# The gate's products on TensorE, beside the arriving weights, in a fused attention, dense and routed layer kernel

## The chip, the cores and the metric

The kernel runs on one core of one Trainium2 chip. The metric is the device time of one execution in microseconds. Engines are TensorE (PE; its weight loads are listed as PEld), VectorE (DVE), ScalarE (ACT), GpSimd (POOL) and SyncE (SP, which here only issues DMAs).

## The reference

Three parts follow each other: gated linear attention, a dense layer pair with squared ReLU, and eight routed experts.

```python
# attention, 4 batches x 8 heads, 768 tokens, 48 columns a head
for t in range(S):
    state = alpha[:, :, t, :, None] * state + einsum('bhd,bhe->bhde', k[:, :, t], v[:, :, t])
    y[:, :, t] = einsum('bhd,bhde->bhe', q[:, :, t], state)
x = y.transpose(0, 2, 1, 3).reshape(3072, 384)
# first mixture
h = maximum(x @ w_in, 0.0)             # w_in 384 x 2048
x = h * h @ w_out                      # w_out 2048 x 384
# second mixture: each expert takes the 384 tokens with the highest logits that are still free
logits = x @ w_gate                    # w_gate 384 x 8
order = argsort(-logits.flatten())
... each token to one expert, 384 tokens to an expert ...
for e in range(8):
    out[mask_e] = maximum(x[mask_e] @ w1[e], 0.0) @ w2[e]     # w1 384 x 1024, w2 1024 x 384
```

## The kernel before

**Units and steps.** The 3072 tokens are 24 chunks of 128; three chunks are a unit (`CPU`, `UT` = 384 tokens), so there are 8 units. The hidden 2048 columns are 16 blocks of 128 (`FT`). A step g is a unit u and a block f, g = 16 u + f. On TensorE step g computes the first layer of block g (`moe_a`, line 390, nine products of 128 x 128 by 128 x 384) and the second layer of block g - 2 (`moe_b`, line 414, nine products). Each value is split into a high and a low float32r part, and a product is three passes over these. Between the two layers lies `moe_ev`: ScalarE's ReLU (line 395), the square (ScalarE in unit 0, VectorE's line 400 in the others), ScalarE's high part (line 401) and GpSimd's low part (line 402).

**Attention** of the next unit runs beside a unit's steps, in pieces (`attn`: decays with two scans on VectorE, lines 229 and 232; scaled keys and queries, 236 and 237; scores on TensorE and masks on VectorE, 255 and 261; keys transposed, 295; results and state, 273, 276, 306 and 312). Three pieces go with four steps. Its PSUM banks come from tag `"a"`, of which there are three.

**Unit 0** is written in order by hand for TensorE, VectorE, ScalarE and GpSimd (`manual_schedule`), up to two steps into unit 1 (`first_step`). In it the first mixture's weights arrive as float64 words, and VectorE narrows them to float32 in three instructions for each block of `w_in` (`conv_in`) and of `w_out` (`conv_out`): lines 351, 353 and 355. Two conversions are started at the end of each step (`start_conv`), the blocks of the first layer two steps ahead of their use. In the next step they are split into high (ScalarE, line 358) and low (GpSimd, line 359). All this keeps the order of the text on each engine. From step 18 on the order is the scheduler's.

**The gate.** The logits are needed before routing starts. For units 0 to 4 VectorE multiplies each chunk's rows (`xo`) by the gate's eight columns, one instruction with a running sum for each expert (`gate`, line 435, a second instruction reads the sum out). From unit 5 (`FUSED`) the second layer's products carry them: `gate_w` multiplies the rows of `w_out` by the gate's weights in the same way (128 such sums, GpSimd adding the two parts into `gx`, line 442) and puts the results as 8 columns beside `w_out`'s 384 (`W` = 392). `share` hands out four steps of this work per step of the units. For that the gate's weights are loaded once, spread to all partitions (`wg`, 128 x 8 x 384). The last unit's logits come from `wlog` and its hidden rows.

**After that** come the search for the experts' thresholds and the experts themselves, in an order by hand.

Of the kernel before, what the change touches and what calls it, by code (L numbers as in the profile page):

```python
# [48 lines left out]
# what each step of an expert does beside its products: s the search of a phase after the next, t the slots  # L49
# of the next, h, p, d weights' parts, x tokens, e, w the former expert's results  # L50
# [21 lines left out]
FUSED = 5  # L72
SHARE = 4
# [14 lines left out]
def moe_kernel(ctx: ExitStack, tc: tile.TileContext, akq, v, w_in, w_out, w_gate, w1, w2, out,  # L88
# [14 lines left out]
    # the last chunk's rows come after one of zeros  # L103
# [14 lines left out]
    # attention inputs of one chunk of 128 tokens: decays, keys and queries with a pair of heads' columns in the  # L118
    # partitions, a column of zeros after each pair's tokens, and values with the tokens in the partitions
# [3 lines left out]
    def load(ch, parts=((0, 3),), eng=sp):  # L123
        """the rows between a pair's heads take the second's first, for whatever is finite will do"""
        for lo, hi in parts:
            for p0, n, r0 in ((0, 64, 0), (64, 48, 48)):
                eng.dma_start(nat[ch % 2][p0:p0 + n, lo:hi, :, :C], akq[ch, r0:r0 + n, lo:hi])
# [4 lines left out]
    # constants that the first chunk needs  # L132
# [30 lines left out]
    # constants that depend on shapes alone  # L163
# [15 lines left out]
    wlog = consts.tile([128, FT, 2, E], F32R, name="wlog")  # L179

# [28 lines left out]
    XF, XT = {}, {}  # L209

    def back(x):
        """a row's elements, the last one first"""
        n = x.shape[-1]
        return bass.AP(tensor=x.tensor, offset=x.offset + n - 1, ap=[list(a) for a in x.ap[:-1]] + [[-1, n]])

    def attn(ch, tags="aaaaa"):
        """yields after each of its parts: a decays, q queries and keys, s scores, n keys back, o results"""
# [7 lines left out]
        # products of the decays from each token on, and up to each token over the whole chunk's; what each pair's  # L225
        # start from comes in where the zeros are
# [41 lines left out]
        def result(lo, hi):  # L268
            """what some pairs of heads give, in one bank"""
# [10 lines left out]
            if cu == CPU - 1 and hi == NP:  # L280
                # the last pair of heads fills the rows that the other pairs leave
# [65 lines left out]
    def narrow(dst, src):  # L347
        """float64 words (low, high) to float32, of which dst takes the bits"""
# [23 lines left out]
    def conv_out(f):  # L372
# [6 lines left out]
        split(lambda i: wout[:, i, f, :DM].rearrange("p (k q) -> p k q", k=KT), r)  # L379
        yield  # L380

# [25 lines left out]
    def moe_b(u, f):  # L407
# [3 lines left out]
        w = W if FUSED <= u < NU - 1 else DM  # L411
# [5 lines left out]
    def moe_out(u, wp):  # L417
        for t in range(CPU):
# [4 lines left out]
            if u >= FUSED:  # L423
                dve.tensor_copy(L[:, c, :], p[:, DM:W])
            else:
                tasks.append(gate(L[:, c, :], xo))
            sp.dma_start(rows(c), xo)

    tasks = []

    def gate(dst, x):
        """x's rows times the gate's weights"""
        for e in range(E):
            junk = gt_.tile([128, DM], F32, name="gj", bufs=1)
            dve.scalar_tensor_tensor(junk, x, 1.0, wg[:, e], op0=OP.mult, op1=OP.mult, accum_out=dst[:, e:e + 1])  # L435
            yield

    def gate_w():
        """w_out's rows times the gate's weights"""
        for f in range(FT):  # L440
            x = gt_.tile([128, DM], F32, name="gx", bufs=2)
            pool.tensor_tensor(x, wout[:, 0, f, :DM].bitcast(F32), wout[:, 1, f, :DM].bitcast(F32), op=OP.add)
            yield from gate(wr[:, f], x)
        split(lambda i: wlog[:, :, i], wr)
        for i in range(2):
            pool.tensor_copy(wout[:, i, :, DM:], wlog[:, :, i])
        yield

    def share(n):
        """n steps of what the vector engine does for the gate"""  # L450
        while n and tasks:
            if next(tasks[-1], "end") == "end":
                tasks.pop()
            else:
                n -= 1

# [14 lines left out]
    def start_conv(n=1):  # L471
        """the next conversions, in turns so that none waits for itself"""
# [13 lines left out]
    for what in ORDER:  # L486
# [15 lines left out]
        if what == "0q":  # L502
# [4 lines left out]
            load_out(0)  # L507
            load_in(1)
# [8 lines left out]
    def logit_range():  # L517
        """the lowest of the logits, but for the last unit's, and what scales them from there to 0..T"""
# [25 lines left out]
    def attend(g):  # L544
        """attention's parts that go with step g"""
# [11 lines left out]
    def first_step(g):  # L557
        """a step of the first unit, whose weights come along"""
# [13 lines left out]
        if g >= 2:  # L572
            moe_b(0, g - 2)
        if g == FT + 1:
            moe_out(0, mp_)
# [9 lines left out]
    gt_, gt_stack = open_pool("gate")  # L585
    wg = gt_.tile([128, E, DM], F32, name="wg")
    sp.dma_start(wg, bass.AP(tensor=w_gate.tensor, offset=w_gate.offset, ap=[[0, 128], [DM, E], [1, DM]]))
    wr = gt_.tile([128, FT, E], F32, name="wr")
    tasks.insert(0, gate_w())

# [665 lines left out]
```

## Time and profile before

| | us |
|---|---|
| median of 3 runs | 973.15 |
| lowest, highest | 966.78, 974.82 |
| span of the profiled execution (its own time is known by the span) | 973.9 |
| TensorE busy | 833.9 |
| VectorE busy | 714.5 |
| GpSimd busy | 443.2 |
| ScalarE busy | 327.7 |

The span runs from the first to the last instruction of the profiled execution. A busy share is a mean over stages that have different limits; a busy TensorE is not TensorE at its peak, since its products are pipelined and the ends of their records are modelled. Times in the rows further down are counted from the span's start.

### The profile page before, as it was taken

What the parts mean: (1) busy time and instruction counts of PE and PEld (TensorE: products, weight loads), DVE (VectorE), ACT (ScalarE), POOL (GpSimd) and SP (SyncE); (2) the same over time, 40 slices, a digit from 0 to 9 for tenths busy, and PEclk for the clock granted to TensorE, in tenths of its full rate; (3) what the DMA queues carried; (4) which work ended last, traced back from release to release, by engine and by line L of the source; (5) the groups of instructions that cost most, each with busy time, mean ns of one, the idle gap of its engine ahead of it and who ended that gap; (6) DMA issues with size and microseconds to landing.
All of it is one profiled execution on the core that took longest, in us unless ns stands there. A gap on an engine that the chain in (4) does not pass through costs nothing.

```text
span 973.9 us, 14629 instructions
## 1 busy us (share of the span) xinstructions
PE 833.9 (86%) x5583; PEld 759.1 (78%) x5583; DVE 714.5 (73%) x1594; ACT 327.7 (34%) x581; POOL 443.2 (46%) x389
## 2 busy tenths in 40 slices
PE   6868779888979889899999999748788797988974
PEld 6658678877878779899999998647677685777974
DVE  6878998999998999958542134777687787875540
ACT  1344533223123223233343352224242442425521
POOL 2386763353454444433342442343464556644431
PEclk7888989999999999999999999958798898988988
DMA  9763543112122122232300000314042240422400
GB/s 208 156 190 107 164 110 70 37 28 61 38 43 62 37 43 61 37 72 56 58 25 1 7 25 13 134 37 155 1 178 102 77 171 9 178 84 96 179 25 27
DMA packets 51484, 76.98 MB, mean 79 GB/s; under 512 B 3409, under 2 KB 42706, under 8 KB 49362
## 3 DMA queue, kind: packets, MB, share of 16 engines
q1 hardware_dynamic: 21570, 27.24, 10.3%
q0 software_dynamic: 5520, 34.61, 9.6%
q10 hardware_dynamic: 24320, 14.16, 7.7%
q8 instruction: 45, 0.74, 0.3%
q14 instruction: 29, 0.24, 0.1%
HBM read 65.27 MB, written 9.54 MB: 77 GB/s over the span
## 4 chain that ended last, share of the span: by engine, by line
PE 40%; DVE 36%; issue 4%; ACT 4%; DMA 1%; POOL 1%; POOLq 0%; DVEq 0%; ACTq 0%
DVE gj L435 15%; PE ph L390 9%; PE p L414 7%; PE ph L957 7%; PE py L975 7%; DVE at L861 3%; PE p L641 3%; DVE s L400 3%; DVE wbuf L922 2%; ACT wbuf L920 2%; DVE A L232 1%; DVE thr L827 1%; DVE cm L829 1%; DVE suf L229 1%; DVE Pt L261 1%
## 5 line engine op out<-in xcount | busy, mean ns | idle before, releaser
L390 PE MATMUL ph<-xT,wbuf 128*128 128x384 f32 x1152 | 234.6, 348 | 29.5 <-DVE s L400 12.0
L390 PEld LDWEIGHTS ph<-xT,wbuf 128*128 128x128 f32 x1152 | 207.5, 192 | 40.4 <-DVE s L400 17.4
L402 POOL TENSOR_TENSOR hl<-s,hl 128x384 fp32r<-128x384 f32 x112 | 141.8, 1266 | 184.9 <-ACT hl L401 171.2
L414 PE MATMUL p<-wbuf,hl 128*128 128x384 f32 (+1 forms) x1008 | 205.4, 348 | 4.9 <-POOL hl L402 2.7
L414 PEld LDWEIGHTS p<-wbuf,hl 128*128 128x128 f32 x1008 | 180.0, 193 | 12.2 <-issue 4.2
L975 PE MATMUL py<-wbuf,hl 128*128 128x384 f32 x576 | 133.6, 364 | 0.0
L957 PE MATMUL ph<-xt,wbuf 128*128 128x384 f32 x576 | 122.5, 358 | 10.3 <-DVE xt L932 5.9
L400 DVE SCALAR_TENSOR_TENSOR s<-ph,s 128x384 f32<-128x384 f32 x112 | 62.0, 553 | 89.2 <-ACT s L395 88.8
L401 ACT ACTIVATE hl<-s 128x384 fp32r<-128x384 f32 x112 | 58.8, 525 | 195.7 <-DVE s L400 193.8
L957 PEld LDWEIGHTS ph<-xt,wbuf 128*128 128x128 f32 x576 | 103.7, 198 | 14.1 <-DVE xt L932 6.7
L975 PEld LDWEIGHTS py<-wbuf,hl 128*128 128x128 f32 x576 | 105.6, 201 | 0.7
L435 DVE SCALAR_TENSOR_TENSOR gj<-gx,wg 128x384 f32<-128x384 f32 x128 | 96.1, 751 | 3.1
L395 ACT ACTIVATE s<-ph 128x384 f32<-128x384 f32 x128 | 62.1, 486 | 100.2 <-PE ph L390 70.5
L435 DVE SCALAR_TENSOR_TENSOR gj<-xo,wg 128x384 f32<-128x384 f32 x120 | 78.3, 652 | 12.9 <-ACT xo L422 10.5
L965 ACT ACTIVATE hl<-ph 128x384 fp32r<-128x384 f32 x64 | 31.7, 496 | 135.6 <-PE ph L957 118.6
L922 POOL TENSOR_TENSOR wbuf<-w2s,wbuf 128x768 fp32r<-128x768 f32 x28 | 53.3, 1925 | 44.1 <-ACT wbuf L920 44.1
L966 DVE SCALAR_TENSOR_TENSOR hl<-ph,hl 128x384 fp32r<-128x384 f32 x64 | 35.4, 553 | 38.3 <-ACT hl L965 37.4
L920 ACT ACTIVATE wbuf<-w1s 128x1024 fp32r<-128x1024 f32 x24 | 52.2, 2227 | 2.3 <-DMA w1s<-in_moe_w_dram,wi 2.3
L983 POOL DMA_INDIRECT out_dram<-o,idx x24 | 29.8, 1243 | 50.9 <-ACT o L980 19.0
L838 PEld LDWEIGHTS <-cm 128*128 128x128 bf16 x210 | 8.1, 100 | 49.9 <-DVE cm L829 46.3
L838 PE MATMUL pc<-oh,cm 128*128 128x32 bf16 x210 | 11.3, 182 | 40.1 <-DVE cm L829 40.1
L729 POOL DMA_INDIRECT xg<-x2d,row x24 | 25.1, 1046 | 38.7 <-DVE idx L785 18.2
(204 smaller groups left out, 1229.8 us busy)
## 6 DMA issues: line engine op xcount, KB each, us to landing
rawi<-in_moe_w_in_dram SPq DMA_DIRECT2D x16, 384.0 KB, 3.5
rawo<-in_moe_w_out_dram SPq DMA_DIRECT2D x16, 384.0 KB, 3.7
akq<-in_akq_dram ACTq DMA_DIRECT2D x16, 384.0 KB, 4.5
akq<-in_akq_dram ACTq DMA_DIRECT2D x16, 288.0 KB, 5.8
x2d<-xo SPq DMA_DIRECT2D x24, 192.0 KB, 2.0
v<-in_v_dram ACTq DMA_DIRECT2D x16, 192.0 KB, 2.5
akq<-in_akq_dram SPq DMA_DIRECT2D x7, 384.0 KB, 5.8
akq<-in_akq_dram SPq DMA_DIRECT2D x7, 288.0 KB, 7.3
```

Of the source, the lines that this page charges most:

```text
L390: pe.matmul(ph[:, :UT], win[:, wi, kt, fs], XT[u][:, xi, kt, :], start=n == 0, stop=n == 3 * KT - 1)
L395: act.activation(s, ph[:, :UT], AF.Relu)
L400: dve.scalar_tensor_tensor(s, ph[:, :UT], 0.0, s, op0=OP.max, op1=OP.mult)
L401: act.activation(hl[:, 0], s, AF.Copy)
L402: (dve if (u, f) == (NU - 1, FT - 1) else pool).tensor_tensor(hl[:, 1], s, hl[:, 0].bitcast(F32), op=OP.subtract)
L414: pe.matmul(PY[u][t][:, :w], hl[:, si, t * C:(t + 1) * C], wout[:, wi, f, :w], start=f == 0 and n == 0, stop=f == FT - 1 and n == 2)
L435: dve.scalar_tensor_tensor(junk, x, 1.0, wg[:, e], op0=OP.mult, op1=OP.mult, accum_out=dst[:, e:e + 1])
L920: act.activation(dst[:, 0], src, AF.Copy)
L922: (dve if "d" in e else pool).tensor_tensor(dst[:, 1], src, dst[:, 0].bitcast(F32), op=OP.subtract)
L957: pe.matmul(ph[:, :CAP], wa[:, wi, kt, j, :], xt[:, xi, kt, :], start=n == 0, stop=n == 3 * KT - 1)
L966: dve.scalar_tensor_tensor(hl[:, 1], ph[:, :CAP], 0.0, hl[:, 0].bitcast(F32), op0=OP.max, op1=OP.subtract)
L975: pe.matmul(PX[k, i][:, :DM], hl[:, hi_, i * 128:(i + 1) * 128], wb[:, wi, j, :], start=j == 0 and n == 0, stop=j == FT2 - 1 and n == 2)
```

## The change

The gate's sums on VectorE go. For each block of `w_out`, in the step in which it is split, TensorE transposes its three 128 x 128 parts into a bank of tag `"a"` and ScalarE copies them out; in the next step's turn TensorE multiplies them by the gate's weights (three products of 8 columns, into the same bank), ScalarE copies the 8 columns beside the high part of `w_out` and VectorE subtracts for the low part. In step 17 GpSimd copies all 8 columns of the 16 blocks to `wlog`. Units 1 to 6 then all have second layers of 392 columns, and VectorE copies the logits from the bank. Unit 0's three chunks take the way of the transposes in unit 1. The gate's weights are loaded as 128 x 24 values on SP's queue ahead of the first mixture's second block. Comments were taken out as well.

```diff
     L = consts.tile([128, NCH, E], F32, name="L")
     wlog = consts.tile([128, FT, 2, E], F32R, name="wlog")
+    wg = consts.tile([128, KT, E], F32, name="wg")
...
         r = t.rearrange("p (q k) -> p k q", k=KT)
         split(lambda i: wout[:, i, f, :DM].rearrange("p (k q) -> p k q", k=KT), r)
+        tasks.append(gate_w(f, r))
         yield
...
-        w = W if FUSED <= u < NU - 1 else DM
+        w = W if u else DM
...
             act.activation(xo, p[:, :DM], AF.Copy)
-            if u >= FUSED:
+            if u:
                 dve.tensor_copy(L[:, c, :], p[:, DM:W])
-            else:
-                tasks.append(gate(L[:, c, :], xo))
             sp.dma_start(rows(c), xo)
+            if not u:
+                tasks.append(first_logits(c, xo))
...
-    def gate(dst, x):
...
-    def gate_w():
...
-    def share(n):
...
+    def by_gate(x):
+
+        pt = bank("a", "pt")
+        for k in range(KT):
+            pe.transpose(pt[:, k * 128:(k + 1) * 128], x[:, k], ident)
+        xt = mp_.tile([128, KT, 128], F32, name="gx", tag="xo", bufs=3)
+        act.activation(xt, pt[:, :DM].rearrange("p (k q) -> p k q", k=KT), AF.Copy)
+        yield
+        for k in range(KT):
+            pe.matmul(pt[:, DM:W], xt[:, k], wg[:, k], start=k == 0, stop=k == KT - 1)
+        yield pt[:, DM:W]
+
+    def gate_w(f, x):
+
+        for r in by_gate(x):
+            if r is None:
+                yield
+        act.activation(wout[:, 0, f, DM:], r, AF.Copy)
+        dve.tensor_tensor(wout[:, 1, f, DM:], r, wout[:, 0, f, DM:].bitcast(F32), op=OP.subtract)
+        yield
+
+    def first_logits(c, x):
+
+        for r in by_gate(x.rearrange("p (k q) -> p k q", k=KT)):
+            if r is None:
+                yield
+        dve.tensor_copy(L[:, c, :], r)
+        yield
+
+    def gates():
+
+        for t in list(tasks):
+            if next(t, "end") == "end":
+                tasks.remove(t)
...
             load_out(0)
+            sp.dma_start(wg.rearrange("p k e -> p (k e)"), w_gate)
             load_in(1)
...
         if g >= 2:
             moe_b(0, g - 2)
+        gates()
         if g == FT + 1:
+            while tasks:
+                gates()
+            for i in range(2):
+                pool.tensor_copy(wlog[:, :, i], wout[:, i, :, DM:])
             moe_out(0, mp_)
         start_conv(2)
...
-    gt_, gt_stack = open_pool("gate")
-    wg = gt_.tile([128, E, DM], F32, name="wg")
-    sp.dma_start(wg, bass.AP(tensor=w_gate.tensor, offset=w_gate.offset, ap=[[0, 128], [DM, E], [1, DM]]))
-    wr = gt_.tile([128, FT, E], F32, name="wr")
-    tasks.insert(0, gate_w())
...
             drain(moe_ev(u, f, ph, hl))
-            share(SHARE)
-            if u == FUSED and f in (0, FT // 2):
-                share(-1)
-                if f:
-                    gt_stack.close()
+            gates()
...
-    a["moe2_w_gate"] = inputs["moe2_w_gate"].reshape(128, KT, E).transpose(2, 1, 0).reshape(E, DM)
+    a["moe2_w_gate"] = inputs["moe2_w_gate"].reshape(128, KT * E)
```

## Rows read from the trace of the kernel before

**Rows 1.** The page: busy time of each engine; the chain's shares by line.

```profile
PE 833.9 (86%) x5583; PEld 759.1 (78%) x5583; DVE 714.5 (73%) x1594; ACT 327.7 (34%) x581; POOL 443.2 (46%) x389
...
DVE gj L435 15%; PE ph L390 9%; PE p L414 7%; PE ph L957 7%; PE py L975 7%; DVE at L861 3%; PE p L641 3%; DVE s L400 3%; DVE wbuf L922 2%; ACT wbuf L920 2%; DVE A L232 1%; DVE thr L827 1%; DVE cm L829 1%; DVE suf L229 1%; DVE Pt L261 1%
```

**Rows 2.** Stretches, units 0 to 5: length, engines' busy time, clock, DMA, GB/s.

```profile
35.40:136.20 100.80, 76.80 (x453) 68.11 (x452) 91.02 (x124) 44.77 (x86) 73.70 (x58) 0.87 0.51 152
136.20:211.90 75.70, 67.94 (x462) 62.59 (x461) 71.44 (x160) 20.02 (x43) 33.15 (x35) 0.95 0.29 58
211.90:291.10 79.20, 67.51 (x449) 61.42 (x450) 75.60 (x185) 20.14 (x45) 36.47 (x32) 0.98 0.22 44
291.10:366.40 75.30, 65.94 (x462) 60.59 (x461) 70.84 (x170) 20.61 (x46) 34.56 (x33) 0.98 0.23 46
366.40:432.80 66.40, 63.78 (x449) 60.12 (x450) 50.77 (x113) 22.26 (x48) 27.80 (x31) 1.00 0.25 52
432.80:496.20 63.40, 63.13 (x462) 60.32 (x461) 41.95 (x92) 21.92 (x45) 24.80 (x28) 1.00 0.26 54
```

**Rows 3.** The same view of the tile `gj` alone (DVE), unit 2.

```profile
211.90:291.10 79.20, 51.73 (x144) 0.98 0.22 44
```

**Rows 4.** Waits in unit 2: in total, how many, the longest.

```profile
ACT hl L401 <- DVE s L400: 52.9, 17, 5.5
```

**Rows 5.** Waits in unit 5.

```profile
DVE s L400 <- ACT s L395: 16.7, 7, 3.3
```

**Rows 6.** Stretches: unit 1 in two parts, and unit 5's first four steps.

```profile
136.20:157.10 20.90, 17.55 (x116) 16.04 (x116) 18.29 (x29) 6.57 (x14) 9.21 (x13) 0.91 0.57 114
157.10:211.90 54.80, 50.39 (x348) 46.55 (x347) 53.15 (x132) 13.46 (x29) 23.93 (x23) 0.97 0.18 36
432.80:447.10 14.30, 14.30 (x106) 13.86 (x105) 10.19 (x23) 6.00 (x12) 4.49 (x6) 1.00 0.43 104
```

**Rows 7.** Timeline (start, duration): small float32 weight loads, around 596 and 693.

```profile
596.34 0.74 PEld L698 LDWEIGHTS pl<-sel,lt 16*128 16x128 f32 x6 [0.26 <-issue]
...
693.28 0.31 PEld L930 LDWEIGHTS px<-ident,xg 128*128 128x128 f32 x3
```

**Rows 8.** Line 424: duration in ns, least, median, most.

```profile
L424 DVE COPY L<-p x6: 160/167/168, 505.0 to 565.2; 128x8 f32<-128x8 f32 x6
```

**Rows 9.** Timeline of steps 6, 7 and 11: narrowing's first instruction, second layer's products.

```profile
81.43 0.36 DVE L351 TENSOR_SCALAR wf<-rawi 128x384 int32<-128x384 int32 x1
...
82.57 1.86 PE L414 MATMUL p<-wbuf,hl 128*128 128x384 f32 x9
...
85.85 1.72 PE L414 MATMUL p<-wbuf,hl 128*128 128x384 f32 x9
...
88.64 0.33 DVE L351 TENSOR_SCALAR wf<-rawi 128x384 int32<-128x384 int32 x1
...
110.10 0.35 DVE L351 TENSOR_SCALAR wf<-rawi 128x384 int32<-128x384 int32 x1
...
112.35 2.03 PE L414 MATMUL p<-wbuf,hl 128*128 128x384 f32 x9
```

**Rows 10.** Timeline of unit 0: line 353, and GpSimd beside it.

```profile
65.19 0.55 DVE L353 SCALAR_TENSOR_TENSOR wfo<-rawo,wfo 128x384 int32<-128x384 int32 x1
...
81.82 1.10 POOL L402 TENSOR_TENSOR hl<-s,hl 128x384 fp32r<-128x384 f32 x1 [1.35 <-ACT hl L401]
...
81.97 1.36 DVE L353 SCALAR_TENSOR_TENSOR wf<-rawi,wf 128x384 int32<-128x384 int32 x1
```

**Rows 11.** Timeline around the end of unit 0.

```profile
133.28 8.11 DVE L232 TENSOR_TENSOR_SCAN A<-akq,whole 112x515 f32<-112x515 f32 x1
...
137.35 1.99 POOL L442 TENSOR_TENSOR gx<-wbuf 128x384 f32<-128x384 f32 x2
```

**Rows 12.** Waits in unit 0 of TensorE's first layer for the splits.

```profile
PE ph L390 <- POOL wbuf L359: 10.1, 8, 3.4
...
PE ph L390 <- ACT wbuf L358: 7.3, 4, 2.3
```

More of the change, by code (lines that the diff above doesn't have):

```diff
@@ L71 @@
 SPLIT = (14, 14, 14)
-FUSED = 5
-SHARE = 4
 SB = 2
@@ L422, in moe_out @@
             act.activation(xo, p[:, :DM], AF.Copy)
-            if u >= FUSED:
+            if u:
                 dve.tensor_copy(L[:, c, :], p[:, DM:W])
-            else:
-                tasks.append(gate(L[:, c, :], xo))
             sp.dma_start(rows(c), xo)
+            if not u:
+                tasks.append(first_logits(c, xo))
     tasks = []
-    def gate(dst, x):
[L433 to L436, printed above, removed]
-    def gate_w():
[L440 to L446, printed above, removed]
-        yield
-    def share(n):
[L451 to L455, printed above, removed]
+    def by_gate(x):
[4 more added lines that the diff above has]
+        act.activation(xt, pt[:, :DM].rearrange("p (k q) -> p k q", k=KT), AF.Copy)
+        yield
+        for k in range(KT):
[18 more added lines that the diff above has]
+                tasks.remove(t)
     order_stack = ExitStack()
```

## Prediction

> **What bounds the kernel now.** I read the page's busy times and its chain first [rows 1]. The tensor engine is busy 86% and the vector engine 73%, which names no bound; the chain does: the largest single entry, 15% of 973.9 us, some 146 us, is the gate's multiply-and-sum on the vector engine (line 435), work that is no part of the big products. Next I cut the trace into the first mixture's units, each from its first product of the first layer to the next unit's [rows 2]. Unit 0 (35.4 to 136.2 us) takes 100.8 us, units 1 to 5 take 75.7, 79.2, 75.3, 66.4 and 63.4. These five do the same products and the same share of attention. In unit 5 the tensor engine is busy 63.13 of 63.40 us at a granted clock of 1.00: 63.4 us is the floor of a unit. In unit 2 the vector engine is busy 75.60 of 79.20 us, 51.73 of them gate work [rows 3]; without that 23.9 us are left, far below the floor. The waits agree: in unit 2 the scalar engine waits 52.9 us in 17 waits for line 400 on the vector engine, which is queued behind gate work [rows 4]; in unit 5 line 400 is itself the waiting one, 16.7 us for the scalar engine [rows 5], so the vector engine has room there. Unit 0 is another regime: the vector engine is busy 91.0 of 100.8 us (weights narrowed from float64, and attention), GpSimd 73.7, the tensor engine 76.8 at a clock of 0.87, a mean of its two levels of 1.2 and 2.4 GHz [rows 2].
>
> **The change, part by part.**
>
> **Units 2 to 4.** All gate work leaves their vector engine (144 instructions in unit 2, each sum being two). What is late next is the tensor engine, as in unit 5, which already has the 392 columns that the change gives to units 1 to 4, so their price is in its 63.4. Removed: 79.2 + 75.3 + 66.4 - 3 x 63.4 = 30.7 us. Unit 5 is at the floor already and gains nothing. The three copies of 8 columns that a unit adds on the vector engine take 0.17 us each [rows 8] and fit beside the products.
>
> **Unit 1** I split at 157.1 us, four steps in [rows 6]. The rest takes 54.8 us against 63.4 - 14.3 = 49.1 in unit 5: 5.7 us, with the vector engine busy 53.15; this goes. The first four steps take 20.9 against 14.3. Of these 6.6 us gate work explains little: a scan on the vector engine lasts 8.11 us, from 133.28, while GpSimd runs one instruction after another, two of them the sums `gx` that the change drops, 1.99 us [rows 11]. I take 2.0 us as gained and leave 4.6. Together 7.7; the bounds are 5.7 and 12.3.
>
> **Unit 0's logits** come to the tensor engine in unit 1, where its time counts: per chunk three transposes, 0.31 us for three in the weight loads, and three products of 8 columns in full float32, which the trace shows as six instructions in 0.74 us [rows 7]. That second row has 16 rows in place of 128, so it is a near row and not the same one. Three chunks by 1.05 us are 3.2 us added, bounds 2 and 5. The copies out of the banks are the scalar engine's, 20 to 22 us busy in a unit [rows 2], and have room.
>
> The Trainium skill (TensorE: Matmul & The Clock Gate, Part 4: PE-mode transpose) gives about 275 ns for a transpose within a kernel. By that price three would take 0.83 us, an estimate, and unit 0's logits 4.7 us; the trace has 0.31 for three, and where they disagree I go by the trace.
>
> **Unit 0.** Each of its 16 steps gets, for one block of the second layer's weights, three transposes, a copy by the scalar engine, and a step later the six instructions, a copy of 8 columns by the scalar engine and a subtraction of 8 columns on the vector engine (for each I take the 0.17 us of line 424 [rows 8]). The tensor engine gets 16 x 1.05 = 17 us of work. Its records cover 76.8 of 100.8 us, so 24 us are open; I count this work at nothing. Were that cover gone it would cost 17 us, and more if the transposes suffer from rows read three words apart, whose price no row of the tensor engine shows.
>
> The price lies in a new wait. The order is written by hand, and the subtraction stands in the vector engine's queue ahead of the next two conversions (lines 351 to 355). It waits for the copy, this for the gate's products, and these stand on the tensor engine behind the attention and the second layer's nine products of that step. So the vector engine may no longer run ahead of the tensor engine: queued behind the wait are the narrowing, then the splits on the scalar engine and GpSimd, then the first layer two steps on. In steps with little of attention the narrowing starts after the second layer's products anyway: in step 7 at 88.64, the products ending at 85.85 + 1.72 = 87.57. In steps that hold attention's results it starts before: in step 6 at 81.43, while the products end at 82.57 + 1.86 = 84.43; in step 11 at 110.10 against 112.35 + 2.03 = 114.38 [rows 9]. With 0.95 us for products and copy, the waits are 3.95 and 5.2 us. In step 6 the tensor engine itself comes some 1.5 us later by the added work, which makes 5.5. After both, the vector engine is busy without a break, so the shift stays: 10.7 us. The 16 subtractions add 16 x 0.17 = 2.7 us. Against that, while the vector engine waits GpSimd runs undisturbed. An instruction of line 353 takes 0.55 us at 65.19 and 1.36 at 81.97, while GpSimd is in line 402 [rows 10]. I take three such meetings, 0.8 us each, as saved in each of the two waits: -4.8. Sum +8.6 us. Bounds: -2 us if the waits fall in time that is lost anyway and the shared access eases; +18 us with no relief, plus the bank that a gate task holds from one step to the next, one of three that attention uses, which may hold up each of three chunks until the vector engine has masked a bank (line 261).
>
> Here the Trainium skill (GPSIMD Engine Reference, Specifications) says that GpSimd shares its SBUF interfaces with the vector engine when that reads two SBUF inputs. The trace agrees by the 0.55 and 1.36 us above. By that rule the subtraction, with one input in PSUM, adds no contention, and the waits lend GpSimd time; without it unit 0 would be 13.4 us longer and the total 951 us.
>
> **Small edits.** The load of the gate's weights goes ahead of a load on SyncE's queue: 12 KB against 384 KB, nothing to 0.5 us. The broadcast load of 1.5 MB goes; no wait named it. Two copies on GpSimd at the end of unit 0 replace two in unit 4 of the same size. I count these at nothing, 0.5 us at most either way. The experts stay as they are.
>
> **Sum.** -30.7 - 7.7 + 3.2 + 8.6 = -26.6 us. The profiled execution has a span of 973.9 us, and its own launch time is not shown apart from that; it lies 0.75 us above the median of the three runs, 973.15. From the median: 947 us.
>
> **The rivals.**
>
> A. Unit 0 swallows the new waits: -30.7 - 7.7 + 3.2 = -35.2 us, 938, and with the whole 12.3 of unit 1 and 2 for the logits -41, 932. For it: the tensor engine waits 17.4 us there for the splits [rows 12], and the shared access gives time back; against it: after both waits the vector engine has no idle time. 0.2.
>
> B. The vector engine pinned to the tensor engine costs the full bound, +18 to +22 us, and the bank shows: -35.2 + 20 = -15, 958 us. For it: one pair of rows doesn't prove the relief. 0.15.
>
> C. Units 2 to 4 don't reach 63.4 because GpSimd's split of the hidden rows (line 402), or the scheduler's new order, is late next. If they stay like unit 4, 66.4 us, 9.0 us are lost: 956 us. Against it: unit 5, with gate work of its own still on the vector engine, is at the floor. 0.1.
>
> D. Slower: every step of unit 0 gets the wait of steps 6 and 11, because the vector engine, once held back, never leads again and meets the tensor engine late each time. 16 waits of (3.95 + 5.2) / 2 = 4.6 us, half of the relief (1.2 us) off each, are 54 us, with the subtractions 57: 973 - 35 + 57 = 995 us. It decides from 35.2 / 16 = 2.2 us lost a step. Against it: conversions are ordered two steps ahead of their use, and in step 7 there is 1.07 us between the products' end and the narrowing [rows 9], enough for the gate's products and the copy. 0.04.
>
> E. The change doesn't do what it says because the vector engine stays the bound in units 1 to 4: 973 us. The 23.9 us left in unit 2 speak against it. 0.02.
>
> **How the numbers follow.** The forecast, 940 to 955 us by its own bounds, has 0.49. With A down to 932 and B and C up to 961 the range leaves out D, E and the tails of A and C, under 2 in 10. A per cent, 9.7 us, is about what a measurement of this kernel can tell from no change (three runs spread over 8 us). Faster by over 1% is below 963.4: the forecast, A, and most of B and C, 0.91; within 1%: the rest of B and C, and E, 0.06; slower 0.03.
>
> **What would show it.** Right: units 2 to 4 at 63 to 64 us each at a clock of 1.00, line 435 gone, line 400 waiting for the scalar engine; unit 0 some 105 to 115 us long with the vector engine waiting for the scalar engine's copy of 8 columns ahead of line 351 in steps that hold attention's results; unit 1 near 71. Wrong: a unit 0 over 120 us, the first layer's waits for the splits above their 17.4 us by more than 10, waits for a bank in tag "a", or units above 66 us with GpSimd's line 402 as the releaser.

## The result, and the profile after

The changed kernel takes 943.03 us (median of four runs, 939.94 to 946.49), the kernel before 973.99 (four runs, 966.78 to 977.53): a ratio of 0.9711, with a 95% interval from 0.9656 to 0.9765. The forecast was 947: the 31 us gained are some 4 more than the 26.6 foreseen. Timed again later, the medians were 946.93 and 972.15, 25.2 us apart. Which part varies so is seen below. The profiled execution took 939.94 us, its span 938.2.

The page after, busy times and the chain's shares by line, beside [rows 1]:

```profile
PE 836.9 (89%) x5754; PEld 773.7 (82%) x5754; DVE 536.1 (57%) x1129; ACT 340.6 (36%) x615; POOL 389.2 (41%) x372
...
PE ph L390 19%; PE p L414 18%; PE ph L962 6%; PE py L980 6%; ACT wbuf L925 3%; PE py L275 3%; DVE wbuf L927 3%; PE py L272 2%; PE psc L254 2%; PE p L646 2%; DVE at L866 2%; DVE cm L834 2%; DMA w1s<-in_moe_w_dram,wi 2%; DVE wfo L350 1%; PE pn L294 1%
```

The vector engine has lost 178 us of work and its 15% of the chain; the first mixture's two layers (lines 390 and 414) lead it now. Lines of attention and conversion stand one lower than before (351 is now 350, 353 is 352, 355 is 354), line 390 to 424 are as they were. New are 435 (transposes), 437 (their copy), 440 (products), 448 (the scalar engine's copy of 8 columns) and 449 (the vector engine's subtraction).

Stretches after, for units 0, 1, 2 and 5, columns as in [rows 2]:

```profile
34.80:146.70 111.90, 88.10 (x590) 80.95 (x589) 87.83 (x142) 52.08 (x117) 65.70 (x60) 0.91 0.45 128
146.70:213.60 66.90, 66.90 (x497) 64.08 (x496) 29.01 (x53) 23.72 (x51) 23.87 (x31) 1.00 0.26 57
213.60:276.90 63.30, 63.30 (x450) 60.66 (x449) 27.43 (x45) 21.51 (x43) 21.52 (x25) 1.00 0.26 55
...
403.30:466.40 63.10, 63.10 (x462) 60.33 (x461) 28.09 (x47) 22.07 (x45) 22.71 (x28) 1.00 0.25 55
```

Units 2 to 4 are at the floor: the tensor engine is busy the whole stretch at a granted clock of 1.00. In unit 2 the scalar engine's wait for line 400, 52.9 us before [rows 4], is small:

```profile
ACT hl L401 <- DVE s L400: 10.5, 15, 1.3
```

Unit 0 is 11.1 us longer, within the forecast's 105 to 115. Unit 1 is 8.8 shorter, 66.9 us where the forecast had it near 71. The unit is a bad cut, though, because what is lost at the end of unit 0 and what is lost in the next four steps change places from one execution to another. I cut instead: **A**, steps 0 to 14 of unit 0; **B**, step 15 and unit 1's first four steps; **C**, the rest of unit 1. Rows A, B of before and A, B, C of after, columns as above:

```profile
35.40:127.40 92.00, 68.80 (x415) 61.07 (x413) 82.22 (x117) 39.34 (x76) 65.21 (x51) 0.89 0.52 150
127.40:157.10 29.70, 25.56 (x153) 23.08 (x154) 27.09 (x36) 12.00 (x25) 17.70 (x19) 0.83 0.54 133
```

```profile
34.80:130.90 96.10, 78.53 (x545) 72.45 (x543) 75.85 (x130) 45.99 (x104) 55.83 (x52) 0.95 0.50 144
130.90:164.80 33.90, 27.67 (x187) 26.12 (x187) 19.91 (x33) 14.24 (x32) 16.24 (x19) 0.85 0.32 70
164.80:213.60 48.80, 48.80 (x358) 46.46 (x357) 21.08 (x33) 15.56 (x32) 17.50 (x21) 1.00 0.19 40
```

Both kernels were profiled again, before once and after twice. Lengths in us:

| stretch | before | after | change of the means | forecast |
|---|---|---|---|---|
| A | 92.0, 91.1 | 96.1, 99.1, 97.7 | +6.1 | +8.6 |
| B | 29.7, 28.2 | 33.9, 33.9, 35.5 | +5.5 | +1.2 (-2.0 and +3.2) |
| C | 54.8, 55.6 | 48.8, 48.8, 48.8 | -6.4 | -5.7 |
| units 2 to 4 | 220.9, 220.8 | 189.7, 189.7, 189.7 | -31.1 | -30.7 |
| unit 7 and on | 416.0, 410.4 | 410.1, 410.2, 415.3 | -1.3 | 0 |

Units 5 and 6 are 0.3 us shorter together. Up to unit 7 the sum is -26.2, the forecast's -26.6 within its scatter.

### The profile page after: what moved, and what is told of

It reads as the page before. It is cut to its first block, busy times and chain, and to the rows that moved or that the text cites. A ratio compares the mean times of both kernels' runs of the same rounds, so it can differ in the third digit from the quotient of the medians.

```text
span 938.2 us, 14520 instructions
## 1 busy us (share of the span) xinstructions
PE 836.9 (89%) x5754; PEld 773.7 (82%) x5754; DVE 536.1 (57%) x1129; ACT 340.6 (36%) x615; POOL 389.2 (41%) x372
## 3 DMA queue, kind: packets, MB, share of 16 engines
q0 software_dynamic: 5520, 34.61, 10.1%
## 4 chain that ended last, share of the span: by engine, by line
PE 66%; DVE 20%; ACT 6%; issue 3%; DMA 2%; POOL 1%; SPq 0%; POOLq 0%; ACTq 0%; DVEq 0%
PE ph L390 19%; PE p L414 18%; PE ph L962 6%; PE py L980 6%; ACT wbuf L925 3%; PE py L275 3%; DVE wbuf L927 3%; PE py L272 2%; PE psc L254 2%; PE p L646 2%; DVE at L866 2%; DVE cm L834 2%; DMA w1s<-in_moe_w_dram,wi 2%; DVE wfo L350 1%; PE pn L294 1%
## 5 line engine op out<-in xcount | busy, mean ns | idle before, releaser
L390 PE MATMUL ph<-xT,wbuf 128*128 128x384 f32 x1152 | 229.9, 343 | 3.0 <-POOL wbuf L358 3.0
L390 PEld LDWEIGHTS ph<-xT,wbuf 128*128 128x128 f32 x1152 | 205.3, 190 | 6.6 <-POOL wbuf L358 5.5
L414 PE MATMUL p<-wbuf,hl 128*128 128x392 f32 (+1 forms) x1008 | 204.6, 347 | 0.0
L402 POOL TENSOR_TENSOR hl<-s,hl 128x384 fp32r<-128x384 f32 x112 | 117.8, 1052 | 195.5 <-ACT hl L401 179.3
L971 DVE SCALAR_TENSOR_TENSOR hl<-ph,hl 128x384 fp32r<-128x384 f32 x64 | 35.4, 553 | 40.9 <-ACT hl L970 40.9
L843 PE MATMUL pc<-oh,cm 128*128 128x32 bf16 x210 | 11.3, 181 | 32.8 <-DVE cm L834 32.8
L927 POOL TENSOR_TENSOR wbuf<-w1s,wbuf 128x1024 fp32r<-128x1024 f32 x13 | 38.3, 2964 | 3.1 <-ACT wbuf L925 3.0
L254 PE MATMUL psc<-qt,kt 48*128 48x128 f32 x384 | 30.8, 301 | 9.4 <-DVE qt L236 5.0
```

Source lines behind the costliest of these rows:

```text
L254: pe.matmul(psc[j][:, p * 128:(p + 1) * 128], kt[o:o + D, p], qt[o:o + D, p], start=True, stop=True)
L390: pe.matmul(ph[:, :UT], win[:, wi, kt, fs], XT[u][:, xi, kt, :], start=n == 0, stop=n == 3 * KT - 1)
L402: (dve if (u, f) == (NU - 1, FT - 1) else pool).tensor_tensor(hl[:, 1], s, hl[:, 0].bitcast(F32), op=OP.subtract)
L414: pe.matmul(PY[u][t][:, :w], hl[:, si, t * C:(t + 1) * C], wout[:, wi, f, :w], start=f == 0 and n == 0, stop=f == FT - 1 and n == 2)
L927: (dve if "d" in e else pool).tensor_tensor(dst[:, 1], src, dst[:, 0].bitcast(F32), op=OP.subtract)
L971: dve.scalar_tensor_tensor(hl[:, 1], ph[:, :CAP], 0.0, hl[:, 0].bitcast(F32), op0=OP.max, op1=OP.subtract)
```

## The experiments

Three questions were open. What does unit 0 pay for: the vector engine's new wait, the tensor engine's added work, or the bank that a gate task holds? What takes the place of the wait? And is the shorter last part the change's?

**The wait in the trace.** Waits in unit 0 after, and step 11's timeline (start, duration):

```profile
DVE wbuf L449 <- ACT wbuf L448: 19.7, 10, 3.5
...
PE psc L254 <- DVE wbuf L449: 4.4, 1, 4.4
...
PE ph L390 <- POOL wbuf L358: 3.0, 7, 1.0
```

```profile
111.99 1.85 PE L414 MATMUL p<-wbuf,hl 128*128 128x384 f32 x9
...
113.68 0.73 PE L440 MATMUL pt<-wg,gx 128*128 128x8 f32 x6
...
114.45 0.18 ACT L448 ACTIVATE wbuf<-pt 128x8 fp32r<-128x8 f32 x1 [0.58 <-PE pt L440]
...
114.66 0.17 DVE L449 TENSOR_TENSOR wbuf<-pt,wbuf 128x8 fp32r<-128x8 f32 x1 [3.47 <-ACT wbuf L448]
114.74 0.41 DVE L350 TENSOR_SCALAR wf<-rawi 128x384 int32<-128x384 int32 x1
```

The second layer's products end at 113.84, the narrowing starts at 114.74: 0.90 us for products and copy, where the forecast had 0.95. There are ten such waits and not two, and the first layer's wait for GpSimd's splits has shrunk, from 10.1 us in 8 [rows 12] to 3.0 in 7. The second row of the waits is one of attention's scores for a bank that the subtraction frees; it falls in B and comes up again below.

**Late split.** The scalar engine keeps the raw products, and one split at the end of unit 0 does all of w_out's, so unit 0's steps hold the tensor engine's gate work and no gate instruction of the vector engine.

```diff
-        act.activation(wout[:, 0, f, DM:], r, AF.Copy)
-        dve.tensor_tensor(wout[:, 1, f, DM:], r, wout[:, 0, f, DM:].bitcast(F32), op=OP.subtract)
+        act.activation(L[:, NCH - FT + f], r, AF.Copy)
...
+            split(lambda i: wlog[:, :, i], L[:, NCH - FT:])
             for i in range(2):
-                pool.tensor_copy(wlog[:, :, i], wout[:, i, :, DM:])
+                pool.tensor_copy(wout[:, i, :, DM:], wlog[:, :, i])
```

> ScalarE puts the 16 blocks' raw products aside, and one split after unit 0 makes both parts of all: VectorE has no gate instruction in unit 0's steps. If VectorE's wait for ScalarE's copy (19.7 us in unit 0) is what unit 0 lost against the kernel before (111.9 against 100.8 us): unit 0 falls to 101 to 104 us and the kernel to about 934. If the bank that a gate task holds from step to step is it: only the bank's release by VectorE is gone, the waits of the transposed keys for the masks stay, 107 to 109 us, 939. If TensorE's added work is it: 111 to 112 us, 943.

Measured: 938.79 us (937.1 to 941.54), 0.9647 of before (0.9575 to 0.9719). Unit 0 is 107.9 us. These are the numbers that were expected if the bank were the loss (107 to 109 us, 939), and not those of the wait theory. The cut tells the two apart only in part: A is 90.3 and B 37.3, so without the wait A is as short as before, and B is no shorter. The wait theory is right on A and was wrong to expect that the whole of unit 0 follows; the bank is taken by itself next.

```profile
35.20:125.50 90.30, 76.26 (x545) 71.00 (x543) 83.42 (x117) 47.29 (x103) 64.16 (x51) 0.96 0.55 153
```

**A bank of its own** for the 8 columns, so that no bank is held from step to step for want of the products. It is still one of the three of tag `"a"`, and it is free again only when the subtraction (line 451 in this run, 449 in the changed kernel) has read it.

```diff
+            if k == 0:
+                pg = bank("a", "pg")
-            pe.matmul(pt[:, DM:W], xt[:, k], wg[:, k], start=k == 0, stop=k == KT - 1)
-        yield pt[:, DM:W]
+            pe.matmul(pg[:, :E], xt[:, k], wg[:, k], start=k == 0, stop=k == KT - 1)
+        yield pg[:, :E]
```

> The products of 8 columns go into a bank of their own that is taken and given back within one step, so that no bank is held from step to step; the subtractions stay. If VectorE's wait is the loss: unit 0 stays at 109 to 112 us, the kernel within 3 us of 943. If the held bank is the loss: the waits of scores and transposed keys for a bank (4.4 and 4.3 us in unit 0) go, unit 0 at 102 to 105 us, the kernel at 935.

Measured: 944.43 us (940.56 to 947.14); unit 0 110.7, A 95.7, B 35.0. As good as unchanged: holding the bank from step to step costs nothing that is seen. This run doesn't take away the wait for the bank that the subtraction frees. The 4.4 us in which attention's products (line 254) waited for line 449 only moved to the next product, line 294, which waits 5.0 us for the same instruction.

**Twice the tensor engine's gate work**: each block's transposes and products are made twice (for the logits of unit 0 too).

```diff
-        for k in range(KT):
+        for k in 2 * list(range(KT)):
             pe.transpose(pt[:, k * 128:(k + 1) * 128], x[:, k], ident)
...
-        for k in range(KT):
+        for k in 2 * list(range(KT)):
```

> Each gate task makes its transposes and its products twice, so TensorE's added work doubles: 17 us more in unit 0 and 3.2 in unit 1. If that work lies beside waits in unit 0: unit 0 up by 3 us at most (1 us later in the three steps where VectorE waits for TensorE), unit 1 by 3, the kernel at 946 to 949. If TensorE's added work is what lengthened unit 0: 12 to 17 us more there and 3 in unit 1, the kernel at 958 to 963.

Measured: 952.43 us (950.82 to 962.2), between the two expectations. The tensor engine's time on the gate's tile `pt`, alone, in A and B of after, then in B and A of this run (columns: its busy time, clock, DMA, GB/s):

```profile
34.80:130.90 96.10, 18.04 (x129) 0.95 0.50 144
...
130.90:164.80 33.90, 6.02 (x44) 0.85 0.32 70
```

```profile
135.50:175.80 40.30, 11.78 (x87) 0.83 0.26 60
34.70:135.50 100.80, 32.47 (x258) 0.93 0.49 137
```

In B 5.8 us more of such work made 5.9 us (40.3 against the mean of 34.4), in A 14.4 us more made 3.2 (100.8 against 97.6). The added work is mostly hidden in A and bare in B. This run has one profile, and the three of the changed kernel spread over 3.0 us in A and 1.6 in B.

**The vector engine copies the 8 columns itself**, past the scalar engine's queue.

```diff
-        act.activation(wout[:, 0, f, DM:], r, AF.Copy)
+        dve.tensor_copy(wout[:, 0, f, DM:], r)
```

> VectorE makes the copy of 8 columns itself, so that its wait is for TensorE's products alone and no longer for ScalarE's queue. If the wait in steps with little attention is for ScalarE's queue (five instructions of the step stand ahead of the copy): VectorE's gate waits fall from 19.7 to 8 to 12 us, unit 0 to 103 to 107, the kernel to about 937. If, as predicted, it is for TensorE: the waits stay at 18 to 21 us, unit 0 at 110 to 113 (16 more instructions on VectorE), the kernel at 943 to 945.

Measured: 940.12 us (933.91 to 945.31). Unit 0 is 112.6 us, A 98.2. The wait is now for the products, in A:

```profile
DVE wbuf L448 <- PE pt L440: 15.7, 6, 7.1
```

The 15.7 us lie between the two expectations (8 to 12 and 18 to 21), unit 0 is where the second put it, and A is no shorter than in the changed kernel. So the scalar engine's queue is a small part of the wait at most: without it the vector engine waits nearly as long for the tensor engine itself, 7.1 us of it in one step.

**Late split and a bank of its own together**, timed twice.

> Raw products of w_out's rows are kept by the scalar engine and split once at the end of unit 0, so the vector engine has no gate instruction in unit 0's steps, and the products have a bank of their own, so that no gate task holds a bank of attention's from step to step. Theory (of unit 0's added time the vector engine's wait costs some 6 us in the first 15 steps, the bank costs nothing, and what is lost from step 15 on comes of low TensorE clock and of scans that meet GpSimd): as with the late split alone, the first 15 steps take 90 to 91 us against 96.1, unit 2 starts at 210 to 212 us against 213.6, median 936 to 940. Rival (the bank is what holds step 15 back once the wait is gone): unit 2 starts at 205 to 207 us, median 932 to 935.

> The kernel with the late split and a bank of its own for the products, timed again beside the changed kernel and the one with later splits of tokens. Theory (the vector engine's wait costs 5 to 8 us of the first 15 steps, and the rest is unchanged): 5 to 8 us below the changed kernel's median of the same turn, so 935 to 938 us. Rival (the difference was scatter of unit 0 and of the last part): within 3 us of the changed kernel.

Measured: 936.75 us (933.62 to 941.11), 0.9634 of before (0.9601 to 0.9667); again 937.10 (934.03 to 939.62), 0.9627 (0.9583 to 0.967). Timed beside it the second time, the changed kernel, whose expectation is

> The changed kernel, unchanged, timed in the same turn as the two others, to compare their medians with it: 940 to 945 us.

took 946.93 us (942.87 to 951.49), more than expected; no run of the one overlaps the other, and 9.8 us lie between the medians, where 5 to 8 were expected. A is 91.0 and 90.8, B 34.3 and 32.8. The medians are those of the theory. Unit 2 starts at 208.5 and 206.4 us, earlier than the theory's 210 to 212 and once within the rival's 205 to 207. B was 37.3 in the one profile of the late split alone, so whether the bank costs something once the wait is gone stays open. This is the lowest median here, and the runs of the late split alone and of the later splits below overlap with it.

**The gate products in one burst** at unit 0's end, none in its steps.

```diff
-        tasks.append(gate_w(f, r))
...
+            for f0 in range(FT):
+                x0 = mp_.tile([128, KT, 128], F32, name="gx", tag="xo", bufs=3)
+                hi, lo = (wout[:, i, f0, :DM].bitcast(F32).rearrange("p (k q) -> p k q", k=KT) for i in range(2))
+                dve.tensor_tensor(x0, hi, lo, op=OP.add)
+                tasks.append(gate_w(f0, x0))
+                gates()
```

> The 16 gate products of w_out's rows leave unit 0's steps and run one behind the other at unit 0's end (the vector engine first adds the two halves of each block again), so that unit 0's steps hold no gate work at all, on any engine. Theory (in unit 0's first 15 steps TensorE's added work lies beside other work): these steps take 89 to 92 us, as in before (92.0) and with the late split (90.3); at the end the 16 tasks cost their own 16 x 1.3 = 21 us on TensorE, so unit 2 starts some 12 to 20 us later than in the changed kernel, and the median is 954 to 964 us. Rival (TensorE's added work is on the path in every step, about 1 us each): the first 15 steps take 82 to 86 us, unit 2 starts within 5 us of 213.6, median 940 to 948.

Measured: 967.68 us (963.95 to 970.08), 0.9964 of before (0.9937 to 0.9991). A is

```profile
34.20:126.10 91.90, 68.76 (x415) 61.02 (x413) 82.08 (x117) 39.31 (x76) 65.28 (x51) 0.89 0.52 150
```

the same as before's 92.0, and no shorter than the 90.3 to 92.3 of the four runs with a late split, which have the tensor engine's gate work in the steps. The theory holds for A, with the price of the burst too low: the tasks alternate between the engines, one task every 1.85 us where 1.3 were counted, and later one every 2.8 us, at a granted clock of 0.50, the lower level. So unit 2 starts at 237.8, 24 us later than in the changed kernel where 12 to 20 were expected, and the median lies above the expected 954 to 964.

**The second half without the first**: one constant of the kernel before, `FUSED = 2` in place of 5. The logits ride as columns from unit 2, while the vector engine still makes all products.

> The kernel before, with one constant changed: the second layer carries the logits as columns from unit 2 on instead of unit 5, and the vector engine still makes all gate products, w_out's rows among them, which must now be done by the middle of unit 2. It is the change's second half without its first. Theory (the tensor engine's products in unit 0 are what pays): the vector engine has 128 + 48 sums of 0.72 us, 126 us, and 24 us of other work a unit to get through from unit 1's start, so units 1 and 2 together take 160 to 175 us against 155 in before, units 3 and 4 drop to 63.3 each, and the median is 955 to 972 us. Rival (it is enough that later units carry the columns): units 1 and 2 take under 145 us and the median is 940 to 950 us.

Measured: 1011.88 us (1006.63 to 1014.67), 1.0386 of before (1.0322 to 1.045): slower, which neither expected.

```profile
244.00:343.20 99.20, 64.32 (x474) 54.67 (x472) 97.36 (x237) 11.15 (x22) 31.16 (x35) 0.60 0.40 75
```

From unit 2's seventh step on the tensor engine waits for the gate's columns; the vector engine is busy 97.36 of 99.2 us, since the attention of units 3 and 4 is drawn into this stretch besides (these units then take 103.7 us together), and the clock granted there is 0.60. The 176 sums took 119.37 us, near the 126 counted; what I missed is that a due date in the middle of unit 2 leaves them nothing to hide under.

**Two of the three splits of unit 1's tokens a step later** (`SPLIT = (14, 15, 15)`), on top of the late split and the bank.

> As the run with the late split and the bank of its own, and two of the three splits of unit 1's tokens (line 328 on GpSimd, one behind the other in step 14) go one step later. In that run one conversion on the vector engine (line 354) took 6.3 us beside GpSimd's unbroken row of six instructions, and step 15 and unit 1's first four steps 34.3 us. Theory (the vector engine is starved as long as GpSimd runs without a gap, and a shorter row lets it go on): that conversion takes under 4 us, step 15 with the four steps takes 30 to 32 us, median 932 to 935 us. Rival (the time goes to the low TensorE clock and to the row of masks and transposes, whatever the conversion does): 34 to 36 us, median 936 to 940 us.

Measured: 937.52 us (934.5 to 943.29). In the trace B is 29.4, in the two runs without this edit 34.3 and 32.8, but the median has not moved, so the time shows no gain. The reason for the edit is seen in the vector engine's conversion beside GpSimd's row; first without the edit (the vector engine's line, then GpSimd's row), then with it (GpSimd's row, then the vector engine's line):

```profile
128.06 6.29 DVE L354 SCALAR_TENSOR_TENSOR wfo<-rawo,wfo 128x384 int32<-128x384 int32 x1
...
128.04 0.99 POOL L358 TENSOR_TENSOR wbuf<-wf,wbuf 128x384 fp32r<-128x384 f32 x1
128.99 1.00 POOL L402 TENSOR_TENSOR hl<-s,hl 128x384 fp32r<-128x384 f32 x1
129.96 1.11 POOL L358 TENSOR_TENSOR wbuf<-wfo,wbuf 128x384 fp32r<-128x384 f32 x1
131.02 2.92 POOL L328 TENSOR_TENSOR xT<-xf,xT 128x384 fp32r<-128x384 f32 x3
```

```profile
130.24 0.99 POOL L358 TENSOR_TENSOR wbuf<-wf,wbuf 128x384 fp32r<-128x384 f32 x1
131.20 1.01 POOL L402 TENSOR_TENSOR hl<-s,hl 128x384 fp32r<-128x384 f32 x1
132.17 1.13 POOL L358 TENSOR_TENSOR wbuf<-wfo,wbuf 128x384 fp32r<-128x384 f32 x1
133.25 1.00 POOL L328 TENSOR_TENSOR xT<-xf,xT 128x384 fp32r<-128x384 f32 x1
...
130.27 4.40 DVE L354 SCALAR_TENSOR_TENSOR wfo<-rawo,wfo 128x384 int32<-128x384 int32 x1
```

GpSimd's row ends at 133.94 and at 134.25, the conversion 0.41 and 0.42 us after it. Shorter row, shorter conversion: that part of the theory holds (4.4 us where under 4 was expected). What was gained in B went elsewhere in this profile: its unit 0 began 2 us later, at 36.5 against 34.4 and 34.0, its A is 92.3 against 91.0 and 90.8, and unit 2 starts at 207.0 against 208.5 and 206.4. Whether that is scatter or the edit's doing, one profile doesn't tell.

**The last part.** Before and after were profiled again.

> The kernel before, unchanged, profiled a second time. Disputed is the last part, from unit 7's first product to the end: 416.1 us in the first profile of before, 410.1 in that of after, though its instructions are the same, and 410.2, 416.4, 421.3 and 407.5 in the four runs with edits of unit 0 alone. Theory (this part varies from one execution to the next by itself): it may come out anywhere from 407 to 421 us, and a value under 414 speaks for it; the time up to unit 7 stays within 2 us of 557.8. Rival (the changed kernel's different history shortens the last part): 415 to 418 us again.

> The changed kernel, unchanged, profiled a second time. Theory (the last part varies by itself): anywhere from 407 to 421 us, over 413 would speak for it; unit 7 starts within 2 us of 528.0. Rival (the last part is shorter by the change): 409 to 411 us again.

Measured: 967.24 and 942.42 us; from unit 7 on 410.4 and 410.2 us. Rows of before, first and second profile:

```profile
557.80:973.80 416.00, 339.28 (x2197) 302.39 (x2195) 270.82 (x683) 148.52 (x213) 183.84 (x129) 0.90 0.24 87
```

```profile
554.90:965.30 410.40, 336.49 (x2196) 299.78 (x2194) 268.06 (x683) 148.54 (x213) 182.49 (x129) 0.91 0.24 88
```

The 410.4 of before speaks for the theory. The 410.2 of the changed kernel would fit the rival as well, but its third profile has 415.3. So this part varies by itself; over all profiles it lies between 407.5 and 421.3 us. Unit 7 starts at 554.9 us in the kernel before, 2.9 us earlier than in its first profile, and at 530.4 in the changed one, 2.4 us later than in its first, so the time ahead of it varies by more than the 2 us expected.

## Why the prediction was right

**Units 2 to 4 and unit 1's rest: right.** 189.7 us are 3 x 63.2 where 63.4 was taken; C fell by 6.4 (forecast 5.7) to 48.8, 0.3 under unit 5's rest of 49.1. The floor read from unit 5 was the whole argument, and it held three times over. Rivals C and E are out.

**Unit 0's cover of the tensor engine: right.** The step "I count this work at nothing" is confirmed in A, though not in B (below): with 18 us of gate work A takes 90.3, 91.0, 90.8 and 92.3 us when the vector engine has no part in it, without any gate work 91.9. Of the next 14.4 us, made by the doubling, 3.2 show.

**The wait of the vector engine: right in kind, and both its terms too small.** Apart from the doubling, nothing else that was changed moves A: with the instruction in the steps A is 95.7 to 99.1 (five profiles), without it 90.3 to 92.3 (five profiles, one of them without gate work), so it costs about 6 us; 8.6 were forecast. That the term came so near is luck in part, since two errors cancel. The two waits of 10.7 us in steps 6 and 11 were measured as 3.07 (the row below) and 3.47 (the row of 114.66 above), and eight more came: 19.7 us.

```profile
82.71 0.17 DVE L449 TENSOR_TENSOR wbuf<-pt,wbuf 128x8 fp32r<-128x8 f32 x1 [3.07 <-ACT wbuf L448]
```

The relief was put at 4.8 us and is larger. The rows of A give it without a model: the vector engine was idle 92.00 - 82.22 = 9.8 us and is idle 96.10 - 75.85 = 20.3; its busy time fell by 6.4 us though it got 2.1 us of new work, so 8.5 us were eased. One line in A, before, after, and with the late split (busy us, mean ns):

```profile
L353 DVE SCALAR_TENSOR_TENSOR wf<-rawi,wf 128x384 int32<-128x384 int32 x14 | 14.3, 1023 | 0.0
```

```profile
L352 DVE SCALAR_TENSOR_TENSOR wf<-rawi,wf 128x384 int32<-128x384 int32 x14 | 8.3, 590 | 0.0
```

```profile
L352 DVE SCALAR_TENSOR_TENSOR wf<-rawi,wf 128x384 int32<-128x384 int32 x14 | 13.4, 957 | 0.0
```

The same instructions take 590 ns while the vector engine is held back and 957 when it runs ahead again beside GpSimd. The forecast's "after both, the vector engine is busy without a break, so the shift stays" is the step that failed: the vector engine does have breaks, eight more waits. I read them so, that once relieved it is early in the plain steps as well and gives the time back there, waiting. Rival D, the wait in every step, came near in number (ten of the thirteen subtractions in A) and not in price: 2 us each, paid for largely by the relief.

The Trainium skill (SBUF — State Buffer, SBUF: two separate sides) calls the pair of ports that the two engines share an exclusive lock, held for a whole instruction. The 590 and 957 ns fit that one blocks the other. By that alone the conversion would have waited for one instruction of GpSimd, about 1 us; the 6.29 us above are a wait through six, and there the measurement decides.

**Unit 1's first steps with unit 0's logits: mis-sized.** This is the term that was wrong: +1.2 forecast, +5.5 measured in B. The tensor engine's busy time there grew from 25.56 and 23.36 us to 27.67, 27.66 and 29.26, by 3.7 between the means, and its idle time by 1.8. Three things bear on it. The logits were well priced, 3.2 us against

```profile
158.57 0.49 PE L435 MATMUL pt<-ident,xo 128*128 128x128 f32 x3
...
159.08 0.82 PE L435 MATMUL pt<-ident,xo 128*128 128x128 f32 x6
...
161.51 0.73 PE L440 MATMUL pt<-wg,gx 128*128 128x8 f32 x6
```

1.31 + 3 x 0.73 = 3.5 us. By the 275 ns of the Trainium skill (TensorE: Matmul & The Clock Gate, Part 4: PE-mode transpose) nine one after the other would take 2.5 us, an estimate. For a single transpose the trace agrees, 272 ns at the median, but the nine overlap and take 1.31 us, so 275 ns is not the price of one in a row:

```profile
L435 PE MATMUL pt<-ident,xo x9: 270/272/273, 158.6 to 159.6; 128*128 128x128 f32 x9
```

But the last w_out tasks run on after A, another 6.02 - 3.5 = 2.5 us of `pt`, and I had covered all of them by unit 0's idle time; the doubled work, 5.9 us longer for 5.8 us more, speaks for next to no cover there in the changed kernel. And the relief came, was larger than the 2.0 us taken, and was met by a new wait. The scan that took 8.11 us before [rows 11] takes 2.14 in the changed kernel, but the subtraction stands behind the scans in the vector engine's queue, and attention's scores wait 4.4 us for the bank that it frees. So it is in all three profiles of the changed kernel; the first:

```profile
134.63 2.14 DVE L231 TENSOR_TENSOR_SCAN A<-akq,whole 112x515 f32<-112x515 f32 x1
...
138.03 0.15 DVE L449 TENSOR_TENSOR wbuf<-pt,wbuf 128x8 fp32r<-128x8 f32 x1
...
138.24 2.07 PE L254 MATMUL psc<-qt,kt 48*128 48x128 f32 x14 [4.41 <-DVE wbuf L449]
```

The forecast had this wait, for a bank of tag "a", among its signs of being wrong, and priced it only in rival B. If relief and wait cancel, 3.5 + 2.5 = 6.0 us stand against the 5.5 measured; that they cancel is argued and not shown. The late split doesn't settle it: there the wait for the subtraction is gone, but a conversion is starved beside GpSimd (the 6.29 us above), and B is 37.3, 34.3 and 32.8 us. With two of GpSimd's splits moved besides, B is 29.4 us, about as before, with all of this gate work in it: so the work itself need not lengthen B.

**The bank and the small edits: right, but for the wait in B.** That a gate task holds a bank from step to step costs nothing measurable while the subtraction stays in place; the 4.4 us above are what rival B feared of the bank, once and not for each of three chunks. Unit 0 starts at 34.8, 34.2 and 34.2 us against 35.4 and 34.1.

**The remaining 4 us.** The first pair of profiles differs by 5.9 us from unit 7 on, which I had not forecast and which is not the change's: the second profile of before has it too. With a gain of 25.2 us in the later timing, the 4 us are no more than this scatter. What makes this part vary was not tried and stays open.

**The sum, in part luck.** Up to unit 7 the -26.2 us are so near the forecast's -26.6 because A came 2.5 us under its term and B 4.3 over it, and C and the later units 1.4 better than theirs.

**Rival A** (938 us) was the forecast without the wait, and a version without it exists: late split and own bank, 937, 35 us below before as rival A summed. It isn't rival A term by term: B is 4.6 us longer there than before, where rival A had +1.2.

## What to carry to other kernels

Work moved to an engine that waits for its input can be had for nothing there, as in A, but its result had better not pass through the engine that sets the pace: in A it was the 8-column subtraction, 0.17 us long, and not 18 us of transposes and products, that cost 6 us. Cheap results can be parked by an engine with room and finished once at the end. When a stretch is cut for a forecast, cut it where lost time cannot change sides, and price the tail of a pipelined task in the stretch where it ends.

## What was not expected of the hardware

With more work the tensor engine's granted clock was higher, not lower: in A this clock, a mean of its two levels, was 0.89 in all four profiles without gate work on the tensor engine (68.8 to 69.0 us busy there) and 0.90 to 0.96 in the ten with it (76.3 to 92.8 us busy). It may be why the added work costs A nothing; that was only argued, not tried.

A vector instruction that meets GpSimd can lose to a whole row of its instructions: 0.55 us became 6.29 beside six of them and 4.40 beside four, and both times the instruction ended 0.4 us after the row did.

Three transposes took 0.57 to 0.61 us where their rows are read three words apart (line 435 from `wfo`; the first three, at a granted clock of 0.52, took 0.91) and 0.49 where they lie in order (from `xo`); 0.31 had been taken for both. Their weight loads (least, median, most in ns):

```profile
L435 PEld LDWEIGHTS pt<-ident,wfo x48: 188/207/262, 42.1 to 146.6; 128*128 128x128 f32 x48
...
L435 PEld LDWEIGHTS pt<-ident,xo x9: 139/141/142, 158.4 to 159.5; 128*128 128x128 f32 x9
```
